# FFT mixing and a SwiGLU block in one kernel: chunk C in both partition halves, and one GpSimd product for both signs of a split unit

## The chip, the cores and the metric

The kernel runs on one core of a Trainium2 chip. The metric is the device time of one execution in microseconds (us). Three runs of the kernel before took 687.03, 688.46 and 688.67 us; their median, 688.46, is the time that the change is held against.

Engine names are those of the profile: PE multiplies matrices (PEld loads its stationary operand), DVE is the vector engine, ACT the scalar engine, POOL is GpSimd, SP issues the transfers.

## What is computed

```python
def _attn_ref(x):                       # x: 8 x 3008 x 256, float32
    X = np.fft.fft(x, axis=1)
    X = np.fft.fft(X, axis=2)
    return X.real.astype(np.float32)

def _moe_ref(x, w_gate, w_val, w_out):  # x: 24064 x 256, d_ff = 1536
    g = x @ w_gate
    silu = g * (1.0 / (1.0 + np.exp(-g)))
    val = x @ w_val
    return (silu * val @ w_out).astype(np.float32)
```

The second function takes the first one's output as 24064 tokens.

## The kernel before

**The mathematics, as far as it is needed.** The real part of the two-dimensional transform is split: the transform along `dim` is folded into the weights (`Wp`, `Wq`, made at the start), the one along `seq` is a product of folded input rows with tables of cosines and sines (`Tab`). For a batch only half of the sequence frequencies k (H = 1504) are transformed; token k and token M - k come from the same two vectors P and Q as "plus" and "minus". So a tile of 512 columns of `Pt` and `Qt` gives 1024 tokens. There are 24 tiles and 8 batches.

**Folding (POOL).** The rows of a batch are loaded four-fold (`X[:, 0:4]` upwards, `X[:, 4:8]` downwards) for two parities q. Chunk A has 128 rows for a parity and fills the partitions (`XA`); chunk C has 60, and before the change two batches share `XC`: an even one in partitions 0 to 63, an odd one in 64 to 127, with both parities side by side in the free dimension. `fold_steps` (L147 to L174) turns them in 7 steps into coefficients: sums and differences (L153), two halves along `dim` (L156, L160), `Af`, then `CE` (L166, L167: for the even frequencies, part 0) and `BB` (L170 to L172: odd ones, part 1). `CE` has an extra column, number 128, which belongs to the first output row alone. The steps are spread over the main loop by `spread` and `fold_at` (L770 to L817); `load_next` hands the next batch's loads to a list from which each unit issues three (`run_loads(3)`, L864), on SP's queue, which also carries the output.

**Transforming (PE, ACT, DVE).** A job is (batch, part). `transform` (L546) makes, for a half `eo`, two PSUM tiles: `v` for q = 0, `g` for q = 1. Each takes two products from chunk A (128 rows) and two from chunk C (64 rows for a batch after the first); part 0 with `eo` 1 adds `row0` (L540), products with a stationary operand of one column. ACT copies the `v` tile to SBUF (`od`, L575), and `put` (L579, "the puts" below) adds and subtracts `od` and `g` on DVE into the columns of `Pt` (`eo` 0) or `Qt` (`eo` 1). `whole_part` does both halves in one go, after the unit that `slot` names: from batch 1's part 1 on, unit f=4 of a tile.

**The main loop** (L851) goes over units (tile t, f): f is one of 12 slices of d_ff. `part_a` makes gate and value for "plus", `part_b`, one unit later, adds `Wm` times Q into the same PSUM tiles, which gives "minus". Between them stand the output matmuls of the tile before (`OWork`, 4 at a time; L676), 24 of which fill a PSUM tile that ACT copies to an `ev` buffer (L682) and SP sends out (L688).

In an ordinary unit DVE multiplies the silu by the value tile for both signs (L744, L762). In a **split** unit (tiles 3 to 22; f in `SPLIT`, or in `SPLIT_END` for tiles 21 and 22) PE leaves the value as an even and an odd part `e` and `o`, DVE makes es, vp and vm (L731, L733, L735), and POOL multiplies (L736 for plus, in `part_a`; L758 for minus, in `part_b`).

Pools that matter: `psG` and `psV` have 3 PSUM tiles each, `psO` has 2; `sgv` and `vv` hold 4 halves each (two split units), `evO` 4 tiles. Every engine takes its instructions in the order of the program; the tile framework adds the waits.

Of the kernel before, what the change touches and what calls it, by code (L numbers as in the profile page):

```python
# [31 lines left out]
def kernel(  # L32
# [66 lines left out]
    XC = const.tile([P, 8, 2, D], F32, name="XC")  # L99
    SDf = const.tile([P, 2, 4, D], F32, name="SDf")  # L100
# [31 lines left out]
    def load_c(b, q):  # L132

        X3 = XC.rearrange("p a q d -> p a (q d)")
        p0 = 64 * (b % 2)
        pm = p0 + NCR
        return ([lambda h=h: q.dma_start(out=X3[p0 + LC * h:p0 + LC * (h + 1), 0:4, :],
                                         in_=up_block(b, JC - LC * h, LC)) for h in range(NC_)] +
                [lambda a=a: q.dma_start(out=X3[p0:p0 + NCR, 4 + a, :], in_=down_set(b, a, JC, LC, NC_))
                 for a in range(4)] +  # L140
                [lambda: q.dma_start(out=XC[pm:pm + 1, 0:4, 1],
                                     in_=rows_at(b, 0, [[R * D, 1], [R * D, 4], [1, D]]))])

    def fold_steps(eng, X, CE, BB, q, r, given=None):  # L147
# [4 lines left out]
        def sd(a, op):  # L152
            tt(SDf[r, a], X[r, 0:4, q, :], X[r, 7:3:-1, 1 - q, :], op=op)  # L153
# [11 lines left out]
        def ce():  # L165
            tt(CE[r, q, :, 0, :], Af[r, :, 0, :], Af[r, :, 1, :], op=Alu.add)  # L166
            tt(CE[r, q, :, 1, :], Af[r, :, 0, :], Af[r, :, 1, :], op=Alu.subtract)  # L167
# [10 lines left out]
    def coef_a(b):  # L178
        if b not in coefA:
            coefA[b] = (cp.tile([P, 2, 2, 2, P + 1], BF16, name="CEa"),  # L180
                        cp.tile([P, 2, 2, 2, P], BF16, name="BBa"))
        return coefA[b]

    def coef_c(b):
        p = b if b < 2 else 1 + b // 2
        if p not in coefC:
            coefC[p] = (cp.tile([P, 2, 2, 2, P + 1], BF16, name="CEc"),
                        cp.tile([P, 2, 2, 2, P], BF16, name="BBc"))
# [33 lines left out]
    nc.vector.memset(XC0, 0.0)  # L222

# [175 lines left out]
    def heads(eng, ev, od, CE):  # L399

        eng.tensor_tensor(CE[:, :, 0, 0, P:P + 1], ev, od, op=Alu.add)
        eng.tensor_tensor(CE[:, :, 0, 1, P:P + 1], ev, od, op=Alu.subtract)
# [132 lines left out]
    def blocks(b, q):  # L535

        p0 = 64 * (b % 2)
        return [(0, slice(0, P), *coef_a(b)), (1, slice(p0, p0 + 64) if b else slice(0, P), *coef_c(b))]

    def row0(b, q, ps):  # L540
        for ch, r, CE, BB in blocks(b, q):
            for kind, cols in ((0, slice(0, GH + 1)), (1, slice(GH + 1, NCE))):
                nc.tensor.matmul(ps[0:1, cols], CE[r, q, 0, kind, P:P + 1], Tab[r, ch, q, 0, cols],  # L543
                                 start=False, stop=True, skip_group_check=True)

    def transform(b, part, eos, given=None):  # L546
        n = NCE if part == 0 else G
        ev, ods = {}, {}
        for q, pool, nm in ((0, psV, "v"), (1, psG, "g")):
            if given:  # L550
                ps = {eo: given[eo][q] for eo in eos}
                blk = []
            else:
                ps = {eo: pool.tile([P, T], F32, name=nm) for eo in eos}
                blk = blocks(b, q)
            for j, (ch, r, CE, BB) in enumerate(blk):
                tab = Tab[r, ch, q]
                for eo in eos:
                    for kind in range(2):
                        if part == 0:  # L560
                            cols = slice(0, GH + 1) if kind == 0 else slice(GH + 1, NCE)
                            l, r_ = CE[r, q, eo, kind, 0:P], tab[:, eo, cols]
                        else:
                            cols = slice(0, G)
                            l = BB[r, q, eo, kind, 0:P]
# [351 lines left out]
```

## Time and profile before

| | before |
|---|---|
| three runs, us | 687.03, 688.46, 688.67 |
| span of the profiled execution, us | 685.5 |
| matmuls of the transform, L567 and L543 | 240 and 64 |
| first and last start of a matmul of L567, us | 45.1 and 612.4 |
| DMA share of q1 (SP's transfers) | 27.4% of 16 engines |
| granted TensorE clock | 1.00 |

The page gives no other time of the profiled execution than its span, from the first to the last instruction; the median of the runs is 3.0 us above it. A line of groups has the program's line, engine, operation and tiles, then the busy time of the group, the mean duration in ns, and the idle time before it with what ended it. A line of the timeline has the start, the duration (of `xN` merged instructions together), engine, line, and tiles.

### The profile page before, as it was taken

To read this page: it belongs to the slowest core of one execution; us is meant where nothing else is said; L and a number is where in the kernel's file an instruction comes from. 1 tells how busy PE (TensorE), PEld (TensorE's weight loads), DVE (VectorE), ACT (ScalarE), POOL (GpSimd) and SP (SyncE) were. 2 spreads that over 40 slices of the span, in tenths; PEclk is the share of its full clock that TensorE was granted. 3 is DMA by queue.
4 is the path that set the end of the run, shared out by engine and by line. 5 is a ranking of instruction groups with operands and counts; after the bars stand their busy time and mean duration, and the time that the engine had idled before them with its cause. 6 is when DMAs were issued, how large, how long until landed. Compare 5 with 4: busy or idle time off the path is not lost.

```text
span 685.5 us, 13259 instructions
## 1 busy us (share of the span) xinstructions
PE 672.8 (98%) x4374; PEld 414.2 (60%) x4374; DVE 514.6 (75%) x919; ACT 432.9 (63%) x764; POOL 579.1 (84%) x565
## 2 busy tenths in 40 slices
PE   8999999999999999999999999999999999999997
PEld 5446655666656566565665566655665656656676
DVE  8896667777777777777777777777786777788862
ACT  7676655666656666565666666655665656656663
POOL 8897987899998999999998989997999555658920
PEclk9999999999999999999999999999999999999999
DMA  9657353324315213335134111125111111101112
GB/s 220 115 77 133 102 138 113 96 76 101 99 32 134 67 51 105 86 71 131 41 76 116 48 32 47 47 58 128 46 48 32 38 40 33 47 31 47 47 48 70
DMA packets 45567, 52.55 MB, mean 77 GB/s; under 512 B 6290, under 2 KB 33466, under 8 KB 45498
## 3 DMA queue, kind: packets, MB, share of 16 engines
q1 hardware_dynamic: 42314, 49.35, 27.4%
q0 software_dynamic: 3184, 2.36, 2.7%
q8 instruction: 34, 0.56, 0.4%
q14 instruction: 35, 0.29, 0.2%
HBM read 29.39 MB, written 24.65 MB: 79 GB/s over the span
## 4 chain that ended last, share of the span: by engine, by line
PE 89%; DVE 5%; issue 2%; POOL 2%; ACT 0%; DVEq 0%; ACTq 0%; POOLq 0%
PE o L676 34%; PE v L716 17%; PE g L716 16%; PE g L753 9%; PE v L753 4%; PE g L567 3%; PE v L567 3%; DVE vv L735 3%; DVE vv L733 1%; PE v L543 1%; PE g L543 1%; PE g L856 1%; PE g L421 1%; PE v L421 1%; PE o L430 0%
## 5 line engine op out<-in xcount | busy, mean ns | idle before, releaser
L736 POOL TENSOR_TENSOR hp<-sgv,vv 128x512 bf16<-128x512 f32 (+1 forms) x126 | 160.1, 1272 | 54.3 <-DVE vv L733 42.4
L676 PE MATMUL o<-Wo,hp 128*128 128x256 bf16 (+2 forms) x1140 | 169.7, 273 | 0.0
L676 PE MATMUL o<-Wo,hm 128*128 128x256 bf16 (+2 forms) x1140 | 169.7, 273 | 0.0
L758 POOL TENSOR_TENSOR hm<-sgv,vv 128x512 bf16<-128x512 f32 (+1 forms) x126 | 159.6, 1272 | 8.5 <-ACT sgv L757 8.1
L676 PEld LDWEIGHTS <-hp 128*128 128x128 bf16 (+2 forms) x1140 | 111.9, 98 | 68.3 <-issue 7.8
L676 PEld LDWEIGHTS <-hm 128*128 128x128 bf16 (+2 forms) x1140 | 111.8, 98 | 64.8 <-issue 4.9
L744 DVE TENSOR_TENSOR hp<-sg,v 128x512 bf16<-128x512 f32 (+2 forms) x162 | 107.9, 666 | 33.2 <-ACT sg L743 32.4
L731 DVE SCALAR_TENSOR_TENSOR es<-bc,w,v 128x512 f32<-128x512 f32 (+1 forms) x126 | 93.7, 744 | 50.5 <-PE v L716 50.3
L762 DVE TENSOR_TENSOR hm<-sg,v 128x512 bf16<-128x512 f32 (+2 forms) x162 | 107.4, 663 | 24.1 <-ACT sg L761 14.4
L761 ACT ACTIVATE sg<-g 128x512 f32<-128x512 f32 (+2 forms) x162 | 94.7, 585 | 45.6 <-PE g L753 45.4
L743 ACT ACTIVATE sg<-g 128x512 f32<-128x512 f32 (+2 forms) x162 | 94.4, 583 | 45.0 <-PE g L716 43.5
L716 PE MATMUL g<-Qt,Wq 128*128 128x512 bf16 (+2 forms) x288 | 108.0, 375 | 0.5 <-DVE Qt L580 0.5
L716 PE MATMUL g<-Pt,Wp 128*128 128x512 bf16 (+2 forms) x288 | 108.1, 376 | 0.1
L716 PE MATMUL v<-Pt,Wp 128*128 128x512 bf16 (+2 forms) x288 | 108.0, 375 | 0.0
L753 PE MATMUL g<-Qt,Wm 128*128 128x512 bf16 (+2 forms) x288 | 108.0, 375 | 0.0
L757 ACT ACTIVATE sgv<-g 128x512 f32<-128x512 f32 (+1 forms) x126 | 75.3, 598 | 47.4 <-PE g L753 41.1
L728 ACT ACTIVATE sgv<-g 128x512 f32<-128x512 f32 (+1 forms) x126 | 75.1, 596 | 40.3 <-PE g L716 35.5
L733 DVE SCALAR_TENSOR_TENSOR vv<-v,es 128x512 f32<-128x512 f32 (+1 forms) x126 | 87.0, 690 | 17.6 <-PE v L753 1.0
L735 DVE SCALAR_TENSOR_TENSOR vv<-v,es 128x512 f32<-128x512 f32 (+1 forms) x126 | 85.7, 680 | 2.7 <-POOL hm L758 2.7
L716 PEld LDWEIGHTS <-Wp 128*128 128x128 bf16 x576 | 56.2, 98 | 41.0 <-issue 4.2
L682 ACT COPY ev<-o 128x512 f32<-128x512 f32 x90 | 52.7, 586 | 30.8 <-PE o L676 28.2
L153 POOL TENSOR_TENSOR SDf<-XA 128x1024 f32<-128x1024 f32 x28 | 66.0, 2364 | 5.2 <-DMA XC<-in_x_dram 3.3
(165 smaller groups left out, 738.0 us busy)
## 6 DMA issues: line engine op xcount, KB each, us to landing
out_dram<-ev SPq DMA_DIRECT2D x96, 128.0 KB
XA<-in_x_dram SPq DMA_DIRECT2D x32, 256.0 KB
XA<-in_x_dram SPq DMA_DIRECT2D x112, 64.0 KB
XC<-in_x_dram SPq DMA_DIRECT2D x32, 120.0 KB
XC<-in_x_dram SPq DMA_DIRECT2D x105, 32.0 KB
out_dram<-ev SPq DMA_DIRECT2D x12, 120.0 KB
out_dram<-ev SPq DMA_DIRECT2D x10, 112.0 KB
XA<-in_x_dram SPq DMA_DIRECT2D x1, 1024.0 KB
```

Source lines behind the costliest of these rows:

```text
L676: nc.tensor.matmul(ps[:n, j, :], hts[minus][:, f, c:c + n], Wo[:, f, :], start=(f == 0), stop=(f == nF - 1))
L716: nc.tensor.matmul(ps[:, :w], Wt[:, gv, fs], src[:, :w], start=start, stop=stop, skip_group_check=True)
L731: stt(es[:, :w], bc[t][:, :w], w0[:, f:f + 1], e[:, :w], op0=Alu.mult, op1=Alu.add)
L733: stt(vp[:, :w], o[:, :w], -0.5, es[:, :w], op0=Alu.mult, op1=Alu.add)
L735: stt(vm[:, w - 1::-1], o[:, :w], 0.5, es[:, :w], op0=Alu.mult, op1=Alu.add)
L736: nc.gpsimd.tensor_tensor(hts[t][0][:, f, :w], sg[:, :w], vp[:, :w], op=Alu.mult)
L743: nc.scalar.activation(sg[:, :w], g[:, :w], AF.Silu)
L744: nc.vector.tensor_tensor(hts[t][0][:, f, :w], sg[:, :w], v[:, :w], op=Alu.mult)
L753: nc.tensor.matmul(ps[:, :w], Wm[:, gv, f * P:(f + 1) * P], Qt[:, :w], start=False, stop=True, skip_group_check=True)
L758: nc.gpsimd.tensor_tensor(hts[t][1][:, f, :w], sg[:, :w], v[:, :w], op=Alu.mult)
L761: nc.scalar.activation(sg[:, :w], g[:, :w], AF.Silu)
L762: nc.vector.tensor_tensor(hts[t][1][:, f, w - 1::-1], sg[:, :w], v[:, :w], op=Alu.mult)
```

## The change

What it does:

1. *Chunk C by parity.* `load_c` puts parity 0 of a batch in partitions 0 to 63 and parity 1 in 64 to 127; two batches stand side by side in the free dimension (`bb`). A batch takes 39 loads of half the size instead of 20. `fold_steps` for C handles both parities of one batch at a time, so that batch 1 needs 7 steps instead of 14 (on half as many partitions). Six loads are issued a unit instead of three while the list begins with loads of C.
2. *Transform in another order.* For a half `eo`, chunk A's products for both q come first, then chunk C's, alternating between q = 0 (rows 0 to 63, into `v`) and q = 1 (rows 64 to 127, into `g`). The `od` copy follows when both are done.
3. *Row 0 with 128 columns.* `CE` has a new layout, [odd | even | zeros], a constant tile for two batches each; `row0` takes the extra column with 127 zeros behind it as its stationary operand. Four POOL memsets at the start write the zeros.
4. *Halves apart.* The two halves of a job run after two units that follow each other, instead of after one.
5. *One POOL product for both signs.* In a split unit `vv` and `sg` have both signs in one tile, `hp` and `hm` are one tile `hpm`; POOL multiplies both signs in one instruction in `part_b`, except for f >= 10, where the plus sign stays in `part_a`. The tile es is gone: `vv[:, 0]` holds it and is overwritten by vp in the third DVE step; vm is the second.
6. *Buffers.* `sgv` and `vv` 3 tiles (6 halves), `evO` 3, `es` none, `bc` in bf16.

```diff
-        p0 = 64 * (b % 2)
-        pm = p0 + NCR
-        return ([lambda h=h: q.dma_start(out=X3[p0 + LC * h:p0 + LC * (h + 1), 0:4, :],
-                                         in_=up_block(b, JC - LC * h, LC)) for h in range(NC_)] +
-                [lambda a=a: q.dma_start(out=X3[p0:p0 + NCR, 4 + a, :], in_=down_set(b, a, JC, LC, NC_))
...
+        bb = b % 2
+        steps = []
+        for qq in range(2):
+            p0 = 64 * qq
+            for h in range(NC_):
+                up = rows_at(b, 2 * (JC - LC * h) - 1 + qq, [[2 * D, LC], [R * D, 4], [1, D]])
+                steps.append(lambda p=p0 + LC * h, up=up: q.dma_start(out=XC[p:p + LC, 0:4, bb, :], in_=up))
+            for a in range(4):
+                down = rows_at(b, R * (a + 1) - 2 * JC + 1 - qq, [[2 * LC * D, NC_], [-2 * D, LC], [1, D]])
+                steps.append(lambda p=p0, a=a, down=down: q.dma_start(out=XC[p:p + NCR, 4 + a, bb, :], in_=down))
...
+    def ce_zero(CE, r, q, kind):
+        return CE[r, q, kind, 2 * P + 1:3 * P + 1]
...
+    for CE in CEs.values():
+        nc.gpsimd.memset(CE[:, :, :, 2 * P + 2:3 * P + 1], 0.0)
...
+    def row0(CE, r, q, ch, qt, ps):
+        for kind, cols in KINDS:
+            nc.tensor.matmul(ps[:, cols], ce_zero(CE, r, q, kind), Tab[r, ch, qt, 0, cols],
+                             start=False, stop=True, skip_group_check=True)
...
+            for eo in eos:
+                for q in range(2):
+                    for kind in range(2):
+                        product(eo, kind, q, coef_a(b), every, q, 0, kind == 0)
+                    if part == 0 and eo == 1:
+                        row0(coef_a(b)[0], every, q, 0, q, ps[eo][q])
+            for eo in eos:
+                for kind in range(2):
+                    for q in range(2):
+                        if b == 0:
+                            product(eo, kind, q, coef_c(b), every, q, 1, False)
                         else:
+                            product(eo, kind, q, coef_c(b), half(q), b % 2, 1, False)
+                if part == 0 and eo == 1:
+                    for kind, cols in KINDS:
+                        for q in range(2):
+                            r = half(q)
+                            nc.tensor.matmul(ps[eo][q][:, cols], ce_zero(coef_c(b)[0], r, b % 2, kind),
+                                             Tab[r, 1, q, 0, cols], start=False, stop=True, skip_group_check=True)
...
-            es = esp.tile([P, T], F32, name="es")
-            stt(es[:, :w], bc[t][:, :w], w0[:, f:f + 1], e[:, :w], op0=Alu.mult, op1=Alu.add)
-            vp = vvp.tile([P, T], F32, name="vv")
-            stt(vp[:, :w], o[:, :w], -0.5, es[:, :w], op0=Alu.mult, op1=Alu.add)
-            vm = vvp.tile([P, T], F32, name="vv")
-            stt(vm[:, w - 1::-1], o[:, :w], 0.5, es[:, :w], op0=Alu.mult, op1=Alu.add)
-            nc.gpsimd.tensor_tensor(hts[t][0][:, f, :w], sg[:, :w], vp[:, :w], op=Alu.mult)
+            vv = vvp.tile([P, 2, T], F32, name="vv")
+            stt(vv[:, 0, :w], bc[t][:, :w], w0[:, f:f + 1], e[:, :w], op0=Alu.mult, op1=Alu.add)
+            stt(vv[:, 1, w - 1::-1], o[:, :w], 0.5, vv[:, 0, :w], op0=Alu.mult, op1=Alu.add)
+            stt(vv[:, 0, :w], o[:, :w], -0.5, vv[:, 0, :w], op0=Alu.mult, op1=Alu.add)
+            if f >= nF - 2:
+                nc.gpsimd.tensor_tensor(hts[t][:, 0, f, :w], sg[:, 0, :w], vv[:, 0, :w], op=Alu.mult)
...
-            nc.gpsimd.tensor_tensor(hts[t][1][:, f, :w], sg[:, :w], v[:, :w], op=Alu.mult)
+            m = slice(1 if f >= nF - 2 else 0, 2)
+            nc.gpsimd.tensor_tensor(hts[t][:, m, f, :w], sg[:, m, :w], vv[:, m, :w], op=Alu.mult)
...
-    spread(("C", 1), 14, 6, 14)
+    spread(("C", 1), 7, 6, 14)
...
-        job_at[u] = jb
+        for eo in range(2):
+            while u in job_at:
+                u += 1
+            job_at[u] = (*jb, (eo,))
...
-        run_loads(3)
+        run_loads(3 if loads and loads[0][0][0] == "A" else 6)
...
-            whole_part(*job_at[i])
+            transform(*job_at[i])
```

More of the change, by code (lines that the diff above doesn't have):

```diff
@@ L99 @@
     XC = const.tile([P, 8, 2, D], F32, name="XC")
+    CEs = {(nm, i): const.tile([P, 2, 2, 3 * P + 1], BF16, name=f"CE{nm}{i}") for nm in "ac" for i in range(2)}
     SDf = const.tile([P, 2, 4, D], F32, name="SDf")
@@ L179, in coef_a @@
         if b not in coefA:
[L180 removed]
+            coefA[b] = (CEs["a", b % 2],
                         cp.tile([P, 2, 2, 2, P], BF16, name="BBa"))
@@ new lines, in product @@
+        def product(eo, kind, q, coef, r, qc, ch, start):
+            CE, BB = coef
+            if part == 0:
+                cols = KINDS[kind][1]
+                l, r_ = ce_main(CE, r, qc, eo, kind), Tab[r, ch, q, eo, cols]
+            else:
+                cols = slice(0, G)
+                l, r_ = BB[r, qc, eo, kind, 0:P], Tab[r, ch, q, (eo + kind) % 2, NOO:NTAB]
+            nc.tensor.matmul(ps[eo][q][:, cols], l, r_, start=start, stop=(ch == 1 and kind == 1), skip_group_check=True)
@@ L572, in transform @@
+        for q in range(2):
             for eo in eos:
@@ L606 @@
     for q in range(2):
-        row0(0, q, acc[1][q])
+        for ch, CE in ((0, CEa), (1, CEc)):
+            row0(CE, slice(0, P), q, ch, q, acc[1][q])
     unfolded(1, 1, SBc, False, True)
```

101 lines of the change are left out of this document (40 added, 61 removed).

## The prediction

> **What bounds the kernel now.** I read the page first (span, busy shares, chain of waits), then the windows for the middle, then the timeline around one transform.
>
> ```profile
> span 685.5 us, 13259 instructions
> PE 672.8 (98%) x4374; PEld 414.2 (60%) x4374; DVE 514.6 (75%) x919; ACT 432.9 (63%) x764; POOL 579.1 (84%) x565
> ...
> PE 89%; DVE 5%; issue 2%; POOL 2%; ACT 0%; DVEq 0%; ACTq 0%; POOLq 0%
> 200.00:300.00 100.00, 99.72 (x643) 60.65 (x642) 76.63 (x134) 63.46 (x111) 97.92 (x89) 1.00 0.29 79
> ```
>
> PE sets the end: 89% of the chain, 99.7 of 100 us in the middle window (columns: PE, PEld, DVE, ACT, POOL). POOL, at 97.9, runs beside it and not ahead of it. But a busy PE is not a full PE: a matmul's record holds its latency, so lost time shows only in the spacing of starts. Part 1 of a job (279.92) and part 0 (308.55):
>
> ```profile
> 279.92 0.48 PE L567 MATMUL v<-Tab,BBa 128*128 128x376 bf16 x2
> 280.33 0.49 PE L567 MATMUL v<-Tab,BBc 64*128 64x376 bf16 x2
> ...
> 282.87 0.49 PE L567 MATMUL g<-Tab,BBc 64*128 64x376 bf16 x2
> 283.30 0.39 PE L716 MATMUL g<-Pt,Wp 128*128 128x512 bf16 x1
> 283.52 0.38 PE L716 MATMUL g<-Qt,Wq 128*128 128x512 bf16 x1
> ...
> 287.43 0.38 PE L716 MATMUL g<-Pt,Wp 128*128 128x512 bf16 x1
> 308.55 0.33 PE L567 MATMUL v<-Tab,CEa 128*128 128x189 bf16 x2
> 308.81 0.34 PE L567 MATMUL v<-Tab,CEc 64*128 64x189 bf16 x2
> ...
> 310.23 0.33 PE L543 MATMUL v<-Tab,CEa 128*1 128x189 bf16 x2
> 311.79 0.39 PE L716 MATMUL g<-Pt,Wp 128*128 128x512 bf16 x1
> ...
> 315.92 0.38 PE L716 MATMUL g<-Pt,Wp 128*128 128x512 bf16 x1
> ```
>
> ```profile
> L567 PE MATMUL g<-Tab,BBc 64*128 64x376 bf16 x28 | 6.9, 325 | 0.0
> ```
>
> One matmul of 376 columns lasts 0.325 and a pair 0.49, so the second starts 0.16 after the first; the next pair, in the other row shape, starts 0.25 after that (280.33 - 279.92 = 0.41). A change of row shape therefore costs 0.25 - 0.16 = 0.09. In part 0 the same reading gives 0.08 and 0.18. Part 1 takes 283.30 - 279.92 = 3.38 us with 8 such changes, part 0 311.79 - 308.55 = 3.24 with 12.
>
> **The transform, on PE alone.** The change does all 128-row products of a half (one `eo`), then all 64-row ones: 2 changes of shape a half. The 64-row products of q = 0 and q = 1 now lie on different row halves and go to different PSUM tiles. Whether two such matmuls overlap, no row of before shows, since a batch's 64-row matmuls all used one row half. Bounds for the second of a pair: nothing, or the full 0.16 (0.08 in part 0). I take 0.02, near overlap: nothing that the two use is shared but the issue.
> - Part 1, a half: 3 x 0.16 + 0.25 for chunk A, 0.17 + 0.02 + 0.25 for C (0.17: the spacing inside a 64-row pair by its 0.49): 1.17. Two halves 2.34 against 3.38: -1.04.
> - Part 0: `eo` 0 is 3 x 0.08 + 0.18 and 0.09 + 0.02 + 0.18, 0.71; `eo` 1 with its row-0 products 7 x 0.08 + 0.18 and 3 x 0.09 + 0.02 + 0.18, 1.21. Together 1.92 against 3.24: -1.32. The row-0 products' weights grow from 1 column to 128 at no cost: their pair (0.33 at L543) already lasts what a full pair does (0.33 at 308.55).
>
> Seven batches have both: 16.5 us. The Trainium skill, "TensorE: Matmul & The Clock Gate", Part 3 (packing small matmuls), says that matmuls on different row groups start about 4 ns apart; no run so far shows it, and by it the sum above would move by less than 1 us.
>
> **What VectorE lets through.** The halves now run after unit f=4 and after unit f=5 instead of back to back. The `od` copy starts only when both q are done, the puts follow it on DVE, and unit 5's split work stands behind the puts. PSUM has 3 `v` and 3 `g` tiles. In the built program's order, half 1's `v` waits for unit 5's first DVE step, and unit 7's `g` for the last put of half 1. The prices:
>
> ```profile
> 309.18 0.47 ACT L575 COPY od<-v 128x377 f32<-128x377 f32 x1 [0.21 <-PE v L567]
> 311.97 1.33 DVE L580 TENSOR_TENSOR Qt<-g,od 128x64 bf16<-128x64 f32 x7 [0.77 <-PE g L543]
> 313.21 0.74 DVE L731 SCALAR_TENSOR_TENSOR es<-bc,w,v 128x512 f32<-128x512 f32 x1
> 283.47 1.07 DVE L580 TENSOR_TENSOR Qt<-g,od 128x304 bf16<-128x304 f32 x3 [0.62 <-PE g L567]
> 284.46 0.74 DVE L731 SCALAR_TENSOR_TENSOR es<-bc,w,v 128x512 f32<-128x512 f32 x1
> 285.33 0.69 DVE L733 SCALAR_TENSOR_TENSOR vv<-v,es 128x512 f32<-128x512 f32 x1
> 285.93 0.68 DVE L735 SCALAR_TENSOR_TENSOR vv<-v,es 128x512 f32<-128x512 f32 x1
> 286.53 0.68 DVE L762 TENSOR_TENSOR hm<-sg,v 128x512 bf16<-128x512 f32 x1
> ```
>
> From start to start: puts 0.99 (part 1) or 1.24 (part 0); es to its dependent 0.87, which is 0.74 + 0.13; independent steps 0.60. The third step now overwrites `vv[:, 0]`, which the second reads, and the built program makes it wait for the second: 0.69 + 0.13 = 0.82 in place of 0.60.
> - Part 1 from half 0's start: last `v` matmul at 0.90, done 1.22, `od` 1.26 to 1.73, puts 1.77, then es, vm, vp, hm at 2.76, 3.63, 4.45, 5.05, puts of half 1 at 5.65, done 6.72; unit 7's `g` at 6.77. Before: 287.43 - 279.92 = 7.51. Gain 0.74, not 1.04.
> - Part 0: `od` 0.80 to 1.27, puts 1.31, then 2.55, 3.42, 4.24, 4.84, puts 5.44 to 6.77; `g` at 6.82 against 315.92 - 308.55 = 7.37. Gain 0.55, not 1.32.
>
> Twelve jobs (part 0 of batches 2 to 7, part 1 of 1 to 6) lie so: 6 x (0.74 + 0.55) = 7.7. Part 0 of batch 1 stands among unsplit units, where PE decides: 1.3. Part 1 of batch 7 follows a split unit, whose hm is not on DVE: 1.0. Transforms: **-10.0**. The Trainium skill, "TensorEngine Tiling (Array Packing)", Performance Considerations, warns that tiling speeds up TensorE but not the emptying of PSUM; these rows bear it out, with 6.5 of 16.5 us kept back.
>
> **The longer split chain elsewhere.** Where two split units follow each other, PE already waits for the third DVE step:
>
> ```profile
> 304.56 0.68 DVE L735 SCALAR_TENSOR_TENSOR vv<-v,es 128x512 f32<-128x512 f32 x1
> 304.82 0.38 PE L716 MATMUL v<-Pt,Wp 128*128 128x512 bf16 x1
> 305.30 0.38 PE L716 MATMUL v<-Qt,Wm 128*128 128x512 bf16 x1
> ...
> 651.25 0.38 PE L716 MATMUL v<-Qt,Wm 128*128 128x512 bf16 x1
> ```
>
> The step ends at 305.24, the matmul starts at 305.30 instead of 0.22 after 304.82. The PE timeline has 24 gaps above 0.2 before this matmul, the last at 651.25, one in each tile from 3 to 20 and six in tiles 21 and 22: 24 x 0.2 = **+4.8**. Bounds: 24 x 0.1 if half of the new wait hides behind its issue, 24 x 0.22. The bf16 `bc` could make es at best as short as the next step, 0.69: 0.05 less each; I take none.
>
> **GpSimd.**
>
> ```profile
> L736 POOL TENSOR_TENSOR hp<-sgv,vv 128x512 bf16<-128x512 f32 x120 | 152.8, 1276 | 47.4 <-DVE vv L733 35.5 <-ACT sg L761 11.9
> L758 POOL TENSOR_TENSOR hm<-sgv,vv 128x512 bf16<-128x512 f32 x120 | 152.4, 1275 | 8.5 <-ACT sgv L757 8.1 <-DVE hp L744 0.4
> L153 POOL TENSOR_TENSOR SDf<-XA 128x1024 f32<-128x1024 f32 x28 | 66.0, 2364 | 5.2 <-DMA XC<-in_x_dram 3.3 <-DMA out_dram<-ev 1.3 <-DMA XA<-in_x_dram 0.5
> ```
>
> Two products, 2.55, become one of 1024 columns, by L153 2.36. POOL is not on the path, and `vv` and `sgv` hold three split units instead of two: zero. Were the product dearer than 2.55, POOL at 97.9 would become the bound. The later hp hurts nothing: a tile's output matmuls start a unit after its last product, and f >= 10 keeps its early one. Four more memsets open the program:
>
> ```profile
> 1.82 0.19 POOL L250 MEMSET putC<- 128x128 f32 x1
> 3.93 1.16 POOL L302 TENSOR_SCALAR t<-kf,mM 128x377 int32<-128x377 f32 x2 [1.12 <-DVE mM L284]
> 5.89 1.83 POOL L302 TENSOR_SCALAR t<-kf,mM 128x377 int32<-128x377 f32 x2 [0.81 <-DVE mM L294]
> ```
>
> At 508 columns, 4 x 0.19 to 4 x 0.19 x 508/128 = 3.0; POOL's idle 1.12 + 0.81 covers 1.9. **+0.3**; uncovered, 3.0.
>
> **SP's queue.** Chunk C's pair of batches takes 78 loads instead of 40, six a unit; the outputs stand behind them.
>
> ```profile
> 61.07 5.43 SPq L137 DMA_DIRECT2D XC<-in_x_dram  x9
> 70.29 2.76 SPq L139 DMA_DIRECT2D XC<-in_x_dram  x3
> 73.15 1.28 SPq L688 DMA_DIRECT2D out_dram<-ev  x3
> 115.00 3.06 SPq L137 DMA_DIRECT2D XC<-in_x_dram  x9
> 90.42 0.59 ACT L682 COPY ev<-o 128x512 f32<-128x512 f32 x1 [0.27 <-PE o L676]
> 96.92 0.59 ACT L682 COPY ev<-o 128x512 f32<-128x512 f32 x1 [0.27 <-PE o L676]
> ```
>
> An output falls due every 6.5 us (96.92 - 90.42). Between two of them now stand about 15 up-loads (0.34 each at 115, 0.60 at 61) and 3 down-loads (0.92), with the output's 1.3: 9.2 us at 0.34, a lag of 2.7 a group, 12 us over the 4.3 groups of a pair. Three `ev` buffers (four before) allow at most 3 x 6.5 - 1.3 = 18. Loads of half the bytes should go at the faster rate: **+1.0**, range 0 to 10 (0.60 gives a lag of 28).
>
> **Sum**: -10.0 + 4.8 + 0.3 + 1.0 = -3.9 us. The profiled span 685.5 becomes 681.6; the median lies 3.0 above the span, so 684.6.
>
> **Rivals.**
> 1. *SP's queue overruns.* Past a lag of 18 an `ev` copy waits on ACT; the activations that free PE's `g` tiles queue behind it, and PE stands. At 0.60 per up-load the first pair's lag is 28, 10 over; at 0.5 it is 22, 4 over, in each of three pairs. For it: 0.60 at 61 us. Against: 0.34 later. With 8.6 us it is 684.6 - 1.0 + 8.6 = 692: slower. It decides from about 7 us of wait.
> 2. *The row halves do not overlap.* Half 0's last `v` matmul comes 0.17 (part 1) or 0.09 later; gains 0.57 and 0.46, plus 0.8 and 0.4 by PE alone: 6 x 1.03 + 1.2 = 7.4, so 687.2, no change. For it: no row shows overlap. Against: separate rows, separate PSUM tiles.
> 3. *DVE does not hold the halves back*, PE's 16.5 all come: 688.5 - 16.5 + 6.1 = 678.1. Against: the built order's waits.
>
> **How the numbers follow.** Forecast 0.50, rival 1 0.27, rival 2 0.10, rival 3 0.08; 0.05 for a slower case not listed. A change of 0.3%, 2.1 us, is about what a measurement can tell. Of the forecast 0.39 lies past that and 0.07 within, 0.04 slower, by its own bounds (the chain 2.4 to 5.3, SP 0 to 10, the head 0 to 3). Faster 0.39 + 0.08 = 0.47, same 0.07 + 0.10 = 0.17, slower 0.36. Range 677 to 695, which reaches to rivals 3 and 1; the forecast's own is 680 to 689.
>
> **What would show it.** In the profile after: 64-row pairs of `v` and `g` starting within 0.05 of each other; a half of part 1 near 1.2 us; half 1's first `v` matmul late by 0.2 to 0.5 behind unit 5's first DVE step; the third split step starting about 0.82 after the second; the gap at the second split unit's last `v` matmul 0.46 instead of 0.26; combined products near 2.36; no long wait of `ev` copies. An `ev` copy waiting on DMA for microseconds, or products above 2.55, would make the prediction wrong, as would a PE that shows no wait for DVE at half 1.

## The result and the profile after

The changed kernel took 699.02 us (median of 4 runs, 698.17 to 701.83) against 687.96 us for the kernel before (4 runs, 687.03 to 688.67). The ratio is 1.0166, with a 95% interval of 1.015 to 1.0181: slower by 11 us, where the prediction said 684.6 and faster. The profiled execution took 701.83 us.

The head of its page and its chain of waits: PE is still the busiest engine, but its share fell from 98% to 95%, POOL's from 84% to 79%, and the chain that ended last now runs through POOL, DMA and SP's queue, which were at 2% or less.

```profile
span 700.1 us, 13151 instructions
PE 668.0 (95%) x4374; PEld 416.9 (60%) x4374; DVE 525.2 (75%) x919; ACT 433.0 (62%) x764; POOL 553.6 (79%) x436
...
PE 68%; DVE 10%; POOL 6%; DMA 5%; issue 5%; SPq 5%; ACT 1%; DVEq 0%; POOLq 0%; ACTq 0%
```

PE's own waits, longest in total first (total us, how often, longest). The first two lines are new; the third stood at 0.4 before, for the step that was then last. The view counts only gaps above 0.15 us: of each gap of some 0.27 in the third line 0.09 was there before, too short to be counted.

```profile
PE o L696 <- POOL hpm L778: 7.5, 4, 2.7
PE g L736 <- ACT sg L781: 6.3, 1, 6.3
PE v L736 <- DVE vv L753: 6.0, 21, 0.6
```

**The transforms did what they should.** The timeline of a part 0 job: half 0 starts at 239.60, half 1 at 242.94, unit 7's gate tile at 246.31.

```profile
239.60 0.33 PE L572 MATMUL v<-Tab,CEa 128*128 128x189 bf16 x2
...
240.02 0.25 PE L572 MATMUL v<-Tab,CEc 64*128 64x189 bf16 x1
240.03 0.25 PE L572 MATMUL g<-Tab,CEc 64*128 64x189 bf16 x1
...
240.30 0.39 PE L736 MATMUL g<-Pt,Wp 128*128 128x512 bf16 x1
...
242.94 0.33 PE L572 MATMUL v<-Tab,CEa 128*128 128x189 bf16 x2 [0.30 <-DVE vv L751]
...
244.14 0.39 PE L736 MATMUL g<-Pt,Wp 128*128 128x512 bf16 x1
...
246.31 0.39 PE L736 MATMUL g<-Pt,Wp 128*128 128x512 bf16 x1
```

The `v` and `g` products of the two row halves start 0.01 apart, and the halves take 0.70 and 1.20 us. From half 0 to unit 7's gate tile it is 6.71 us, against 7.37 before. The same reading of a part 1 job gives 6.65 against 7.51:

```profile
211.64 0.48 PE L572 MATMUL v<-Tab,BBa 128*128 128x376 bf16 x2
...
212.79 0.39 PE L736 MATMUL g<-Pt,Wp 128*128 128x512 bf16 x1
...
218.29 0.38 PE L736 MATMUL g<-Pt,Wp 128*128 128x512 bf16 x1
```

Read like this, the fourteen jobs of batches 1 to 7 took 10.6 us less in all: 0.80 to 0.85 less in each of the six part 1 jobs, 0.24 to 0.73 in the six of part 0, and 1.15 and 1.05 in the two that lie otherwise.

**What went wrong begins on SP's queue.** The timeline of SP's queue, POOL, ACT and PE around 110 us:

```profile
63.08 6.92 SPq L140 DMA_DIRECT2D XC<-in_x_dram  x15
...
85.61 0.59 ACT L702 COPY ev<-o 128x512 f32<-128x512 f32 x1 [0.27 <-PE o L696]
92.50 1.09 SPq L708 DMA_DIRECT2D out_dram<-ev  x3
93.64 3.55 SPq L143 DMA_DIRECT2D XC<-in_x_dram  x4
97.23 5.55 SPq L140 DMA_DIRECT2D XC<-in_x_dram  x15
102.83 3.53 SPq L143 DMA_DIRECT2D XC<-in_x_dram  x4
106.40 0.64 SPq L145 DMA_DIRECT2D XC<-in_x_dram  x1
107.14 2.12 SPq L129 DMA_DIRECT2D XA<-in_x_dram  x6
108.43 4.64 POOL L165 TENSOR_TENSOR SDf<-XC 128x1024 f32<-128x1024 f32 x2 [7.69 <-DMA XA<-in_x_dram]
109.36 1.15 SPq L708 DMA_DIRECT2D out_dram<-ev  x3
...
115.39 0.59 ACT L702 COPY ev<-o 128x512 f32<-128x512 f32 x1 [8.17 <-DMA XA<-in_x_dram]
115.88 0.60 ACT L781 ACTIVATE sg<-g 128x512 f32<-128x512 f32 x1
116.53 0.56 PE L736 MATMUL g<-Pt,Wp 128*128 128x480 bf16 x1 [6.31 <-ACT sg L781]
117.28 0.61 PE L736 MATMUL v<-Pt,Wp 128*128 128x480 bf16 x1
```

Chunk C's 78 loads for batches 2 and 3 keep the queue until 107.0. Before, the last of 40 ended at 88.45, as this row of the kernel before shows:

```profile
87.81 0.64 SPq L141 DMA_DIRECT2D XC<-in_x_dram  x1
```

So two things are late. One is the fold on POOL, which waits 7.69 us for rows of `XC` (the view names other loads of the same queue). The other is the outputs. Up to 92.50 there were 18 loads between two outputs, as the prediction had it. Then the pair's first fold asks for all that is left of its loads (`run_loads` in `fold_step`), so 24 loads of C, and 6 of A behind them, go out between the outputs at 92.50 and 109.36. The output of the copy at 85.61 is issued 23 us after it. With three `ev` buffers the next `ev` copy waits 8.17 us on ACT, `sg` queues behind it, and PE stands for 6.3. That is the mechanism of the prediction's first rival, at one place.

The second half of the loss is later. PE waits four times for POOL's combined product: 1.32 us at 172.77, 2.72 at 203.55, 1.09 at 315.80 and 2.36 at 346.36. Before the two long ones POOL itself has waited 5.08 and 5.90 us for A rows; their loads stood in the queue behind those of the next pair's chunk C (the view names an output of that queue):

```profile
189.66 2.35 POOL L165 TENSOR_TENSOR SDf<-XA 128x1024 f32<-128x1024 f32 x1 [5.08 <-DMA out_dram<-ev]
...
201.15 2.34 POOL L778 TENSOR_TENSOR hpm<-sgv,vv 128x1024 bf16<-128x1024 f32 x1
203.55 0.50 PE L696 MATMUL o<-Wo,hpm 128*128 128x256 bf16 x3 [2.72 <-POOL hpm L778]
204.72 0.63 PE L736 MATMUL v<-Qt,Wm 128*128 128x512 bf16 x1
...
346.36 0.50 PE L696 MATMUL o<-Wo,hpm 128*128 128x256 bf16 x3 [2.36 <-POOL hpm L778]
```

The three longest stops also cost clock: a matmul of 512 columns that lasts 0.38 lasts 0.63 for 3 to 6 us behind them. Behind the stops of 1.32 and 1.09 the granted clock stayed at 1.00. The windows (columns: PE, PEld, DVE, ACT, POOL, PEclk, DMA share, GB/s) show it below 1 there, and in the head of this execution:

```profile
10.00:20.00 10.00, 8.14 (x30) 3.66 (x29) 7.71 (x14) 7.18 (x14) 9.17 (x16) 0.83 1.15 216
100.00:120.00 20.00, 13.67 (x86) 8.04 (x85) 10.64 (x25) 7.38 (x14) 7.82 (x6) 0.89 0.44 99
200.00:220.00 20.00, 17.24 (x103) 9.73 (x102) 12.88 (x23) 9.36 (x17) 19.06 (x16) 0.91 0.11 35
```

The split chain is longer as forecast: the second of these two matmuls starts 0.65 after the first instead of 0.48.

```profile
513.71 0.38 PE L736 MATMUL v<-Pt,Wp 128*128 128x512 bf16 x1
514.36 0.38 PE L736 MATMUL v<-Qt,Wm 128*128 128x512 bf16 x1 [0.27 <-DVE vv L753]
```

A rough account of the profiled span (+14.6 us; this execution is the slowest of the four): transforms -10.6, the split chain +3.0 (such gaps, as far as they exceed the usual 0.22, add up to 9.6 us against 6.6 before; 21 of the long ones are left of 24), the `ev` wait +6.3 and half clock to 122.2 behind it (5.7 us at half speed) +2.8, the four output waits +7.5 and half clock behind two of them (3.4 us each) +3.4, the head +1.4. That is +13.8; the other 0.8 is not accounted for.

### The profile page after: what moved, and what is told of

The parts are those of the page before. It is cut to its first block, busy times and chain, and to the rows that moved or that the text cites. A ratio compares the mean times of both kernels' runs of the same rounds, so it can differ in the third digit from the quotient of the medians.

```text
span 700.1 us, 13151 instructions
## 1 busy us (share of the span) xinstructions
PE 668.0 (95%) x4374; PEld 416.9 (60%) x4374; DVE 525.2 (75%) x919; ACT 433.0 (62%) x764; POOL 553.6 (79%) x436
## 3 DMA queue, kind: packets, MB, share of 16 engines
q0 software_dynamic: 3184, 2.36, 2.3%
## 4 chain that ended last, share of the span: by engine, by line
PE 68%; DVE 10%; POOL 6%; DMA 5%; issue 5%; SPq 5%; ACT 1%; DVEq 0%; POOLq 0%; ACTq 0%
PE o L696 27%; PE g L736 14%; PE v L736 13%; PE g L772 6%; DVE vv L751 3%; PE v L772 3%; POOL hpm L778 3%; PE v L572 3%; DVE vv L752 2%; DVE vv L753 2%; DMA XC<-in_x_dram 2%; POOL SDf L165 2%; DMA out_dram<-ev 2%; DMA XA<-in_x_dram 2%; SPq L143 1%
## 5 line engine op out<-in xcount | busy, mean ns | idle before, releaser
L778 POOL TENSOR_TENSOR hpm<-sgv,vv 128x1024 bf16<-128x1024 f32 (+2 forms) x126 | 291.9, 2322 | 73.7 <-ACT sgv L776 63.6
L696 PE MATMUL o<-Wo,hpm 128*128 128x256 bf16 (+3 forms) x2280 | 342.5, 274 | 7.5 <-POOL hpm L778 7.5
L696 PEld LDWEIGHTS <-hpm 128*128 128x128 bf16 (+3 forms) x2280 | 224.8, 99 | 146.9 <-issue 18.7
L751 DVE SCALAR_TENSOR_TENSOR vv<-bc,w,v 128x512 f32<-128x512 bf16 (+1 forms) x126 | 93.7, 744 | 57.8 <-PE v L736 53.2
L782 DVE TENSOR_TENSOR hpm<-sg,v 128x512 bf16<-128x512 f32 (+2 forms) x162 | 107.3, 663 | 31.9 <-ACT sg L781 22.5
L763 DVE TENSOR_TENSOR hpm<-sg,v 128x512 bf16<-128x512 f32 (+2 forms) x162 | 107.6, 664 | 30.9 <-ACT sg L762 29.1
L752 DVE SCALAR_TENSOR_TENSOR vv<-v,vv 128x512 f32<-128x512 f32 (+1 forms) x126 | 87.0, 690 | 13.8 <-DVE vv L751 0.9
L753 DVE SCALAR_TENSOR_TENSOR vv<-v,vv 128x512 f32<-128x512 f32 (+1 forms) x126 | 86.9, 690 | 4.3
L736 PEld LDWEIGHTS <-Wq 128*128 128x128 bf16 x450 | 44.2, 98 | 31.7 <-issue 8.2
L772 PE MATMUL v<-Qt,Wm 128*128 128x512 bf16 (+2 forms) x162 | 60.9, 376 | 2.1 <-DVE hpm L763 2.1
L736 PE MATMUL v<-Qt,Wq 128*128 128x512 bf16 (+2 forms) x162 | 60.2, 372 | 0.0
```

What stands on the lines that cost most here:

```text
L696: nc.tensor.matmul(ps[:n, j, :], hts[:, minus, f, c:c + n], Wo[:, f, :], start=(f == 0), stop=(f == nF - 1))
L736: nc.tensor.matmul(ps[:, :w], Wt[:, gv, fs], src[:, :w], start=start, stop=stop, skip_group_check=True)
L751: stt(vv[:, 0, :w], bc[t][:, :w], w0[:, f:f + 1], e[:, :w], op0=Alu.mult, op1=Alu.add)
L752: stt(vv[:, 1, w - 1::-1], o[:, :w], 0.5, vv[:, 0, :w], op0=Alu.mult, op1=Alu.add)
L753: stt(vv[:, 0, :w], o[:, :w], -0.5, vv[:, 0, :w], op0=Alu.mult, op1=Alu.add)
L763: nc.vector.tensor_tensor(hts[t][:, 0, f, :w], sg[:, :w], v[:, :w], op=Alu.mult)
```

## The experiments

All times are medians; the kernel before, run beside each, was at 687.7 to 688.3. Lines of an experiment's kernel lie up to two off those of the changed kernel.

### Are the products late by themselves, and is it the queue?

**f = 9 early again.**

```
-            if f >= nF - 2:
+            if f >= nF - 3:
...
-            m = slice(1 if f >= nF - 2 else 0, 2)
+            m = slice(1 if f >= nF - 3 else 0, 2)
```

> Only f = 9's plus product is early again (f >= nF - 3 in place of f >= nF - 2), so that a split unit 9 has two GpSimd products of 512 columns. Theory (late product): the output matmuls of the next tile reach row f = 9 before POOL has made the combined product; the four waits of PE for POOL at L696 (1.49, 2.88, 1.26 and 2.53 us, 8.2 together, and some 1.5 of half clock behind them) go, and the median falls from 699.0 to 688.5 to 691.5. Rival (POOL's backlog as a whole): POOL is simply behind at these places, and one product more (18 x 0.23 us) leaves it as far behind; the waits stay or move to other rows, and the time stays at 697 to 701.

696.61 us (692.6 to 697.64), 2.4 less than the changed kernel. Neither theory: the output wait at 172 went, but at the same place PE then waited 3.47 us for a gate tile, since an `ev` copy stood 5.33 us for an output on SP's queue. One late party had hidden another.

**C loads four a unit, first folds eight units later.**

```
-    lo = 25
+    lo = 33
...
-        run_loads(3 if loads and loads[0][0][0] == "A" else 6)
+        run_loads(3 if loads and loads[0][0][0] == "A" else 4)
```

> Chunk C's 78 loads of a pair go out four a unit instead of six, and the first pair's folds begin at unit 33 instead of 25, so that no burst of loads is forced at unit 25. Theory (SP's queue): the ev copy that waited 8.17 us at 115.39 no longer waits, PE's 6.5 us at 116.53 and the half clock after it (some 2 to 2.5 us) go, 699.0 to 690 to 692. Rival (the wait belongs to POOL and DMA latency, not to the number of loads ahead of the output): the ev copy still waits for microseconds somewhere between units 14 and 34, and the time stays above 696. The later folds also move POOL's work by 8 units, so the POOL waits at 172.77 and 203.55 may move by up to 2 us in all, either way.

706.35 us, 7.3 slower than the changed kernel. The `ev` wait at 115 did go, but the theory's time was wrong: POOL's work was only put off. POOL stood idle first and was too late afterwards. PE's waits at L696 from 167 to 209 us grew to 5.36, 2.18 and 3.48 us, and at 200 it waited another 4.48 for a value tile.

```profile
110.44 2.22 POOL L778 TENSOR_TENSOR hpm<-sgv,vv 128x960 bf16<-128x960 f32 x1 [13.73 <-ACT sgv L776]
...
194.78 2.34 POOL L165 TENSOR_TENSOR SDf<-XA 128x1024 f32<-128x1024 f32 x1 [14.09 <-DMA out_dram<-ev]
```

So POOL's early time is worth as much as the queue's. The pace and the start were changed together here; a pace of four also stands in the fast kernels below, so it is not a loss by itself.

**Half of chunk C's loads on ACT's queue.**

```
         for qq in range(2):
+            q = nc.scalar if qq and b > 1 else nc.sync
...
+        steps = [s for two in zip(steps[:len(steps) // 2], steps[len(steps) // 2:]) for s in two]
```

> From batch 2 on, the loads of chunk C's upper half (20 of a batch's 39) go out on ACT's queue in place of SP's, one of each in turn; nothing else is changed. Theory A (SP's queue is the root of both losses: it makes the ev copy wait, and it lands the loads late, so that POOL's folds wait at 108.43, 189.66 and 333.50 and its products come late): both the ev wait and the four output waits go, 699.0 to 682 to 688. Theory B (the combined product is late by itself): only the ev wait of 8.2 us and the half clock behind it go, the output waits stay at 5 us or more, 689 to 692. Theory C (20 issues of some 0.4 us on ACT delay its activations by as much as SP gains): 696 or above, with ACT idle time before DMA issues in place of the ev wait.

715.68 us: theory C, though not shown to be the whole of it. An issue holds the engine's own instructions back. Ten issues in a row, 6.5 us of them, kept an activation waiting for 6.95 us:

```profile
87.19 2.21 ACTq L141 DMA_DIRECT2D XC<-in_x_dram  x5
90.28 3.62 ACTq L144 DMA_DIRECT2D XC<-in_x_dram  x4
...
94.69 0.60 ACT L764 ACTIVATE sg<-g 128x512 f32<-128x512 f32 x1 [6.95 <-DMA XC<-in_x_dram]
```

The Trainium skill, "DMA: Bandwidth & Descriptors", section "Issuing engines are not separate DMA queues", says that initiating DMAs on several engines saves only the sequencer's time to initiate them, "which is usually small relative to the DMA itself". Here that time is what binds: the 78 loads of the first pair took 38.5 us of SP's queue in the changed kernel. On ACT an issue took about as long (2.21 / 5 and 3.62 / 4 above), but stood between activations. The run has a second effect: SP's own A loads waited 26.9 us in all between 40 and 90 us for loads of `XC`, the outputs came late behind them, and PE stood for 5.9 us at 86.65. How much of the 16.7 us belongs to which was not tried.

**The old split unit and four `ev` buffers** (es in its own tile, two products of 512 columns), the rest as changed:

> The split unit as in the kernel before (es in its own tile, one early and one late product of 512 columns, four vv and sgv tiles of one product), four ev buffers; the transforms, the layout and the loads as in the changed kernel. What it gives back: the split chain (-4.3 to -4.8), and by four ev buffers up to 6.5 of the 8.17 us that the ev copy waits. Theory A (POOL is late because the loads are): POOL still waits for loads at 67 and 108 and has 120 x 0.23 = 27 us more products, so that output or gate waits of 2 to 6 us stay, 684 to 690. Theory B (the combined product is the cause): no wait of PE for POOL is left, 677 to 683.

689.69 us (10 runs, 687.18 to 693.46), ratio to the kernel before 1.0037 (1.0019 to 1.0054). Theory A in kind, at the upper end of its range: the chain's waits and the `ev` wait went, and one fold that waits for its loads now costs PE a single stop of 7.1 us, besides two of 2.2 and 1.0:

```profile
187.88 2.34 POOL L165 TENSOR_TENSOR SDf<-XA 128x1024 f32<-128x1024 f32 x1 [12.41 <-DMA out_dram<-ev]
...
192.22 0.59 PE L737 MATMUL v<-Pt,Wp 128*128 128x512 bf16 x1 [7.11 <-DVE vv L756]
```

**Both of the last edits:**

> The last two edits together: the old split unit with four ev buffers, and half of chunk C's loads on ACT's queue. Both theories: all that the change lost is back but the head's 1.4 us, the transforms' gain of 7.7 to 10 stays: 688.2 - 10 + 1.4 = 679.6, from 677 to 683. If it is no faster than 688 the gain in the transforms is lost elsewhere, and the prediction's -10.0 is wrong too.

719.78 us. Far off, with the losses of the run before it: an activation waited up to 11.2 us behind issues on ACT. It says nothing about the transforms.

**The zero blocks' memsets behind POOL's angles:**

> The four memsets of the zero blocks stand behind POOL's angles and the first weight loads in place of ahead of them. Theory (the memsets delay POOL's part of the head): the first matmul of the first unit comes 1 to 1.5 us earlier, back to where it was before, and the time falls by as much, to 697.5 to 698. Rival (the head's 1.4 us come from the clock, halved at 13.6 to 16.5 us, or from 128-column row-0 weights): the first unit stays where it is and the time within 0.5 of 699.0.

698.92 us, the rival's time, but the first unit did not stay where it was. Its gate matmul starts at 28.29 instead of 26.45: in their new place the memsets delay a step of POOL's tables, and PE waits 3.52 us for it instead of 1.64. Why the median did not follow is open, so this run does not price the memsets. The changed kernel's own trace does: after them POOL reaches the step behind the angles at 7.74 us, against 7.70 before, so their 1.9 us fit into its idle time. And the head's 1.4 us go with the granted clock from 10 to 20 us, which differs between executions of the same head: where it is 0.83, as in the changed kernel's trace, the first gate matmul of a kernel with the memsets in front and these blocks of rows starts near 26.5; where it is 1.00, as in the first two runs under the next heading, at 24.8, 0.4 ahead of the kernel before (25.19).

### The loads in another order

From batch 2 on, chunk A is folded first and chunk C's pair after it, an A batch's loads go to the front of the list, and C loads go four a unit. No work is added or removed.

```
-    lo = 25
+    lo = 27
...
-        spread(("C", b), 14, lo, (lo + u) // 2)
-        spread(("A", b), 14, (lo + u) // 2 + 1, u)
+        spread(("A", b), 14, lo, (lo + u) // 2)
+        spread(("C", b), 14, (lo + u) // 2 + 1, u)
...
-                loads.extend((("A", b + 1), fn) for fn in load_a(b + 1, nc.sync))
+                loads[0:0] = [(("A", b + 1), fn) for fn in load_a(b + 1, nc.sync)]
...
-        run_loads(3 if loads and loads[0][0][0] == "A" else 6)
+        run_loads(3 if loads and loads[0][0][0] == "A" else 4)
```

> Only the order of loads and folds is changed, from batch 2 on: chunk A of a pair's first batch is folded first (units 27 to 45 for batch 2) and chunk C's pair after it, a batch's A loads go ahead of what waits in the list, and C loads go out four a unit; the work and the number of loads are the same. Theory A (the 78 C loads land too late for a fold that stands early, so POOL waits, its products come late, and the outputs queue behind a burst): POOL's waits for loads at 108.43, 189.66 and 333.50 go, the ev copy's 8.2 us and PE's four output waits go with them, 699.0 to 680 to 686. Theory B (the combined product is late by itself): only the ev wait goes, 689 to 692. If POOL stands idle for more than 8 us before unit 27, the later start can bring output waits back, as moving the folds from 25 to 33 did, and the time stays at 692 or above.

687.72 us (10 runs, 686.66 to 689.45): 11.3 us less than the changed kernel, by order and pace alone, and level with the kernel before, ratio 1.0003 (0.999 to 1.0015). It lies between the theories: the long `ev` wait and the long waits for loads from 189 us on went, two output waits stayed, and POOL stood for 11 us until the first A rows of batch 2 were there. Whether this order would help the kernel before was not run; behind the head, its PE had no wait for POOL that it could save. PE's waits and POOL's:

```profile
PE v L736 <- DVE vv L753: 6.8, 24, 0.6
PE o L696 <- POOL hpm L778: 4.7, 2, 3.6
...
99.20 4.67 POOL L165 TENSOR_TENSOR SDf<-XA 128x1024 f32<-128x1024 f32 x2 [11.13 <-DMA XC<-in_x_dram]
```

**The same with the old split unit and four `ev` buffers:**

> The old split unit with four ev buffers (689.7 us by itself) and chunk A before chunk C. Theory A: its waits of 7.27 us at 192.22, 2.36 at 169.76 and 1.19 at 289.62 came from folds that waited for loads and go: 689.7 to 677 to 681, by the transforms' gain below the kernel before. Theory B (with 27 us more of products POOL is too slow whatever the loads do): the waits move to other tiles, 686 or above.

680.67 us (680.19 to 682.32), ratio 0.9895 (0.9878 to 0.9912): theory A, and faster than both kernels. With the loads in this order points 5 and 6 of the change thus cost 687.72 - 680.67 = 7.0 us. Of PE's waits there are left:

```profile
PE o L697 <- POOL hpm L757: 1.6, 1, 1.6
PE v L737 <- DVE vv L756: 1.4, 3, 0.7
```

**Blocks of 12 rows in chunk C** with the old split unit and the old order of loads (`LC, NC_ = 12, NCR // 12`, three loads a unit):

> The old split unit with four ev buffers, and chunk C's rows laid in blocks of 12 (LC = 12) in place of 4: 37 loads for a pair of batches in place of 78, of the same bytes; C first, as in the changed kernel. The up-loads of 16 rows took 0.35 to 0.46 us of SP's queue and the down-loads of 60 rows 0.88 to 0.92. If an issue costs by its rows (some 0.18 + 0.0117 a row), an up-load of 48 rows takes 0.74 and a pair 20 x 0.74 + 16 x 0.9 + 1.3 = 30 us of queue in place of 38 to 40; POOL's wait for C loads of 7.6 us near 108 goes and the time falls from 689.7 to 683 to 687. If an issue costs by the load, an up-load stays at 0.4 and a pair takes 24 us, 679 to 684. If the queue's time is not what holds POOL, it stays at 689 to 691.

682.50 us, 7.2 less than with blocks of 4. The pair's four groups of five up-loads of 48 rows took 3.20, 2.56, 2.05 and 2.12 us, 0.50 a load; in the changed kernel the four groups of 15 loads of 16 rows took 6.92, 5.28, 5.22 and 5.55, 0.38 a load. Three times the rows and bytes cost 1.3 times the queue, so the issue costs mostly by the load, and the pair is done at 92.4 instead of 105.

```profile
79.74 2.05 SPq L140 DMA_DIRECT2D XC<-in_x_dram  x5
...
91.77 0.62 SPq L145 DMA_DIRECT2D XC<-in_x_dram  x1
```

The head became 3 us slower with it: a gate matmul that starts at 50.33 in the run above starts at 53.37 here. In the trace the products that place chunk C's rows of batch 0 (`o<-XC,putC`) start at 18.26 instead of 15.31; the blocks change these loads too. What of it is theirs was not tried.

**Order and blocks of 12 together** (three loads a unit):

> The old split unit with four ev buffers, chunk A before chunk C, and blocks of 12. Theory A: the loads were no longer late without blocks of 12, so it is at e15's time within 1.5 us, 676 to 681. Rival (SP's queue still binds after the reordering): another 2 to 4 us below e15.

684.10 us, outside both: 3.4 slower than the order alone. No gain from the queue shows, and the head was again later, by 4.4 us at the first gate matmul (29.24 against 24.8).

### The terms, once nothing is late

These three start from the kernel at 680.67, the fourth from the one at 687.72.

**The third DVE step in place** (es written to vp's tile, vm from it, vp last):

> The old split unit, four ev buffers and chunk A before chunk C (680.7 us), but the third DVE step of a split unit in place again, as the change has it: es is written to vp's own tile, vm is made from it, and vp last, over es. Theory (the in-place third step waits for the second): the 24 gaps of 0.256 us before a second split unit's last v matmul become 0.435, + 4.3 us, 684 to 686. Rival (the gap hides elsewhere once nothing else is late): 680 to 682.

689.11 us (10 runs, 687.59 to 690.02), + 8.4: more than either said. From start to start the spacing at the second split unit's last `v` matmul grew from 0.47 to 0.68, about as in the theory; over all such places it adds up to 6.0 us more. (The line below stood at 1.4 before, but the view leaves out gaps under 0.15, as most of these were.) In this form es also needs a `vv` tile that POOL must first give free: DVE's first step now waits 9.1 us for POOL in 14 places. So a part of the 8.4 is not the chain's.

```profile
PE v L737 <- DVE vv L755: 10.2, 30, 0.7
```

**The row halves not used side by side** (`half(0)` in place of `half(q)`):

> The old split unit, four ev buffers and chunk A before chunk C, but q = 1's 64-row products use row half 0 as well (chunk C's share of q = 1 is then made from q = 0's rows). Here nothing else is late, so that the row halves' overlap can be priced. Theory (the prediction's rival 2): 16.5 us of transforms lose 7 x (2 x 0.15 x 2 + 2 x 0.07 x 2 ...) = 6 us of PE alone, of which DVE's hold hides over half: + 2 to + 3.5 us, 682.7 to 684.2. If DVE holds nothing: + 5.5 to + 6.5, 686 to 687. If DVE hides all: within 0.7 of 680.7.

684.70 us, + 4.0: the overlap is worth that, between the cases in which DVE hides over half of it and nothing. (q = 1's rows are not read, so a part of the output differs; the amount of work is the same.) The same edit on the changed kernel:

> The 64-row products of q = 1 use row half 0 like those of q = 0, so that no two matmuls lie on different row halves (chunk C's share of q = 1 is then computed from q = 0's rows: that part of the output differs). Theory (row halves overlap, spacing 113 ns against 209 a matmul): PE's transforms grow by 0.15 x 8 = 1.2 us a part 1 job less what the waits for DVE hide; with the prediction's gains that is +2.6 us, 701.6, and at most 7 x (0.6 + 0.7) = +9. Rival (the overlap is worth nothing since the halves wait for DVE anyway): 699.0 within 1.

701.48 us, + 2.5, near what was expected, but other waits had shrunk in it (the gate wait from 6.3 to 4.6 us), so the cleaner run decides.

**Both halves after the same unit:**

> The old split unit, four ev buffers and chunk A before chunk C, with both halves of a transform after the same unit. Theory (DVE holds the halves apart; spreading them over two units is what lets PE keep part of its gain): PE waits 0.65 (part 1) and 0.89 us (part 0) for the puts at the next gate tile in each of 12 jobs, as in the run that did this to the changed kernel, less the 0.47 and 0.2 us waits of the spread halves that go: + 2 to + 6 us, 683 to 687. Rival (the waits are the same wherever the halves stand): within 1 of 680.7.

684.21 us, + 3.5, inside the theory's range. PE waits for the puts at the next gate tile, 13 times:

```profile
PE g L737 <- DVE Pt L604: 7.5, 13, 0.7
```

On the changed kernel it could not be told:

> Both halves of a transform after the same unit again, back to back, and everything else as in the changed kernel. Theory (DVE holds the halves apart, as the prediction has it): the two halves' PE work closes up to 2.3 and 1.9 us, but unit 5's split work and unit 7's gate tile wait for four puts in a row; this costs at most what the spread layout lost (its waits of 0.47 and 0.2 to 0.25 us a job), and the time stays within 3 us of 699.0. Rival (the second half's split units after unit f = 5 are what pushes POOL and DVE late): the time falls by more than 4 us.

702.31 us with runs from 695.97 to 703.1: no gain, and the loss is about as large as the spread.

**f = 9 early, with chunk A before chunk C:**

> The changed kernel with chunk A before chunk C (687.7 us), and f = 9's plus product early as well. Theory (what is left of the late product: two waits of PE for POOL at L696, 4.7 us, most of it at 164): they go or shrink below 1 us, 682.5 to 685. Rival (POOL is late at 164 by its backlog, not by the combined product of f = 9): a wait of 2 us or more stays at 160 to 175 at an output or a gate tile, 686 or above.

683.91 us, - 3.8, in the theory's range, though a wait of 2.5 us stayed at 163, now for the early product, as the rival had it. So the late product costs 3.8 us even where the later load waits are gone: 2.3 us of PE's waits, and some 1.7 of clock, which was 0.76 from 163 to 170 behind the stop of 3.6 us and 1.00 behind that of 2.5. What stays may come from POOL's 11 us of waiting at 99; that was not tried.

## Why the prediction was wrong

- **PE sets the end, and lost time shows in the spacing of starts:** right.
- **The transform on PE alone:** right. Halves of 1.17, 0.71 and 1.21 us were forecast; 1.15, 0.70 and 1.20 came. The 0.02 for the second of a pair was at most 0.01, so the second rival was out; its price was too low, though (2.6; measured 4.0).
- **What VectorE lets through:** right: -10.6 instead of -10.0. Unit 7's gate tile was forecast 6.77 and 6.82 us after half 0, and came after 6.65 and 6.71. A part of the nearness is luck: the part 0 job that was read for the time before, 7.37, is 0.07 longer than the other five of its kind. That the halves wait at all speaks against the third rival (0.30 us at 242.94); that spreading them pays is shown by + 3.5 us when they are put together.
- **The longer split chain, + 4.8:** right for one gap, too much in sum. The third step starts 0.73 after the second instead of the forecast 0.82 (from 242.99 to 243.72 in the rows below), and the gap grew by 0.18 instead of 0.2. But behind PE's long stops DVE has caught up and the gap is missing, so the changed kernel's trace has + 3.0 us. Where nothing else is late the in-place step cost 8.4 us, of which the extra `vv` tile is a part that was not separated. DVE's timeline in the changed kernel:

```profile
242.15 0.74 DVE L751 SCALAR_TENSOR_TENSOR vv<-bc,w,v 128x512 f32<-128x512 bf16 x1
242.99 0.69 DVE L752 SCALAR_TENSOR_TENSOR vv<-v,vv 128x512 f32<-128x512 f32 x1
243.72 0.69 DVE L753 SCALAR_TENSOR_TENSOR vv<-v,vv 128x512 f32<-128x512 f32 x1
```

- **"The later hp hurts nothing: a tile's output matmuls start a unit after its last product, and f >= 10 keeps its early one":** this step failed. It looked at the order of the program and took POOL to be on time. The product itself took 2.32 us, as forecast (2.36), but POOL had no slack to be on time with: its share in the middle was 97.9 us of 100 before. When a fold waits for loads, f = 9's product is behind it, and the output matmuls reach row 9 first: 7.5 us of waits in four places, about 3.4 us of clock, and 3.8 us even with the loads in order.
- **Head + 0.3:** right for the memsets, whose 1.9 us POOL's idle time took in. The 1.4 us seen go with the clock of that execution.
- **SP's queue, + 1.0 (0 to 10):** the main failure, and not by the rate. An up-load took 0.38 us over the four groups of the first pair (0.46 in the first), near the 0.34 that was taken, although the reason given for it was wrong: half the bytes made a load no cheaper (3.06 / 9 = 0.34 at 115 before, 4.14 / 12 = 0.35 at 148.27 after). What failed is the layout of the queue. The step let 18 loads stand between any two outputs, but the fold's own demand sends all that is left at once, 24 of C with 6 of A behind them, and the lag reached 23 us, past the 18 that three buffers allow. So the first rival's mechanism came, though not by its rate, and once instead of three times: 6.3 us of wait and 2.8 of clock. That this is near the rival's 8.6, for which it shows no working, is luck. And the step asked only who stands behind the loads in the queue, not who waits for the data: chunk C's pair came 19 us later (107.0 against 88.45) for a fold whose slot had not moved, and the A rows behind the next pairs came late in turn. That put POOL behind, and through it the combined products. Another order and pace of loads and folds gives back 11.3 us.

So the range, 677 to 695, reached the rival's 692 but not two failures at once. POOL's lateness and SP's have one cause, the loads of chunk C, and had been priced as if apart, one of them at zero. How the 11.3 us divide between the `ev` wait and POOL stays open, since each hid part of the other in the run with f = 9 early.

## What to carry to other kernels

When a change splits transfers, count the issues and what one holds its queue for, then follow both the work that stands behind them and the work that waits for their data, with its slot. A result that is made later is free only as far as its engine has slack: read that engine's idle time where it is needed, not the program's order. And fold or load first what is cheap to load: moving ready work forward, at a slower pace of loads, was worth 11.3 us here; putting it off cost 7.3.

## What the runs showed of the hardware

- In the first pair an up-load of 16 rows of 1 KB held SP's queue for 0.38 us, one of 48 rows for 0.50, and one of 60 down-rows for some 0.9 (3.53 / 4). Rows of 2 KB instead of 1 KB made no difference (0.34 and 0.35).
- A stop of PE of 2 to 3 us may bring the half clock or not. Behind the stop of 2.72 us at 203.55 matmuls of 512 columns lasted 0.63 until 207.7, behind the one of 6.3 us those of 480 columns lasted 0.61 until 122.2. Over all the runs here, past the head, the 24 stops of 1.0 to 1.8 us were followed by a clock of 1.00. Of 13 stops of 2.1 to 3.0 us that began at or near full clock, seven were followed by half clock for a time (the shortest 2.11, in the run with loads on ACT's queue) and six were not (the longest 2.96, in the run with both of those edits). All 17 of 3.2 us and more were. The Trainium skill, "TensorE: Matmul & The Clock Gate", Part 1 (the HAM clock gate), gives one idle window of about 3.4 us as the limit, on a window that runs freely; the long stops agree with it, the seven short ones lie below.
- Products of different row halves, into different PSUM tiles, start 0.00 to 0.01 us apart.
